# Sums of exponentials over agents: TensorE products with ones replaced by GpSimd reductions in pairs 6 to 25

## The chip, the cores and the metric

One Trainium2 chip, one of its cores. The metric is the device time of one execution in microseconds (us), measured from outside the program; three executions of the kernel before gave 986.49, 987.38 and 988.31 us. Times inside the kernel come from one profiled execution.

## The reference

Two batches of 12480 queries, keys and values with 128 channels, and 49 agents per batch, all float32. Then a feed-forward layer with 2048 hidden units and a leaky rectifier follows.

```
a2k     = softmax(agents @ k.T / sqrt(128))      # over the keys
agent_v = a2k @ v                                # 49 x 128
q2a     = softmax(q @ agents.T / sqrt(128))      # over the 49 agents
x       = q2a @ agent_v                          # 24960 x 128
h       = x @ w_in
out     = (max(h, 0) + alpha * min(h, 0)) @ w_out
```

## The kernel before, in words

The kernel never forms x. For each batch it folds agent_v into the first layer's weights, `sa` and `sb` (a value and what rounding left of it), so that h is the exponentials of the query scores times `sab`. The softmax of a query needs a division by the sum of its 49 exponentials; since the layer is positively homogeneous that division is done last, on the output rows.

The 24960 queries are cut in 52 groups of 480, and two groups make a **pair** k (0 to 25). A pair's tiles are 128 x 960: group 2k in the first 480 columns, group 2k+1 in the other 480. Partitions 0 to 63 hold the agents once and partitions 64 to 127 hold them again (49 are real, the others give exp = 0), so that two products with 64 rows each can go through the two halves of TensorE at the same time.

The main loop runs over 416 **steps** s, eight for each group, 16 for each pair; pair k begins at step s0 = 16 k. In step s the loop issues, in this order: what was put in `first` for the step (by `pre`), `g1(s + 2)`, what was put in `plan` for the step (by `at`), and `g2(s)`. Each engine works through its own instructions in that order, so the order of the text is the schedule.

- `g1` (lines 958 to 978): six products (64 rows, 480 columns each) into the two halves of a PSUM tile `h` (two such tiles), then ScalarE's `rh` = relu(h) (L974) and VectorE's `rl`, what rounding left of it (L975). L975 has one operand in PSUM and one in SBUF.
- `g2` (980 to 1008): twelve products of `rh` and `rl` into the group's accumulator (L990). In a group's last step three more products (L1001), ScalarE's copy (L1006) and VectorE's sum (L1007) close the group.
- The output of group g: `o_take` (a 32 x 32 block transpose on VectorE, L1012), `o_scale` (VectorE, times the reciprocal, L1017: two operands in SBUF) and `o_store` (four DMAs on SyncE's queue, L1035), at steps (g+1)*8 plus 4, 5 and 6, from `OUT`.
- The softmax of pair k, steps relative to s0 from `CHAIN`: `q_transpose` (VectorE, -18), `q_hi` (ScalarE) and `q_lo` (VectorE, two operands in SBUF, L845; both -16), `q_logits` (eight products, -14), `q_take` (ScalarE copy, -13), `q_swap` (two DMAs on SyncE's queue that swap the halves, L883, -13), `q_add` (VectorE, L890, -11), `q_max` (GpSimd's reduction over the partitions, L894, -10), `q_sub` (VectorE, L899, -7), `q_exp_hi` and `q_exp` (ScalarE, -6 and -5), `q_split` (VectorE, two operands in SBUF, L912, -5), `q_sum` (four products with a matrix of ones, L923, +4), `q_spread` (ScalarE copies the sums out of PSUM, L933, and a DMA on SyncE's queue puts them in the order of the output, L939; +5) and `q_rec` (three small instructions on VectorE, L946 to L951, +10).

Beside the pairs the keys of the second batch are worked on in steps 16 to 88 and its values in steps 96 to about 190 (`KEYS`, `VALUES`: `k_exp_a` L618, `v_split` L609 and `k_exp_c` L632 on VectorE, with two operands in SBUF each); steps 189 to 206 fold them into the second batch's weights. Pairs 1 to 5 lie mostly beside the keys, 6 to 12 beside the values, and 13 to 25 have the loop to themselves (called the late pairs below).

Of the kernel before, what the change touches and what calls it, by code (L numbers as in the profile page):

```python
# [9 lines left out]
F32 = mybir.dt.float32  # L10
F32R = mybir.dt.float32r
U32 = mybir.dt.uint32
AF = mybir.ActivationFunctionType
ALU = mybir.AluOpType
# [9 lines left out]
VALUES = ((((0, 3, 1, 1), (3, 1, 4, 4)), 6), (((3, 0, 7, 8), (2, 8, 5, 6)), 10))  # L24
FOLD = (189, 195, 198, 202, 205, 206)
CHAIN = (-18, -16, -16, -14, -13, -13, -11, -10, -7, -6, -5, -5, 4, 5, 10)
CHAIN_0 = (-19, -18, -18, -11, -9, -6, 1, 6, 10, 15, 17, 19)
CHAIN_1 = (-14, -13, -13, -11, -10, -10, -10, -10, -8, -7, -5, -5, 4, 5, 10)
EARLY = (1, 3, 6, 6)
OUT = (4, 5, 5)  # L30


LAGS = (7, 12, 17, 20, 21, 24)
# [22 lines left out]
def kernel(  # L56
# [11 lines left out]
    nc = tc.nc  # L68
# [4 lines left out]
    P = 128  # L73
    HALF = 64
    NF = DFF // P
    GT = 480
    TB = GT // 32
# [13 lines left out]
    SCALE = 1.0 / math.sqrt(C)  # L91
# [5 lines left out]
    p1 = ctx.enter_context(tc.tile_pool(name="p1", bufs=1))  # L97
    p2 = ctx.enter_context(tc.tile_pool(name="p2", bufs=2))
# [11 lines left out]
    def pair_tile(name, i=None):  # L110

        i = (step[0] // NM + 1) % 2 if i is None else i
        return late[i].tile([P, 2, 512], F32, tag="x", name=name)
# [21 lines left out]
    padb = const.tile([P, 1], F32, name="padb")  # L135
# [654 lines left out]
    NGT = B * NG  # L790
    gq = {}
# [20 lines left out]
    def flat(t):  # L812
        return t.rearrange("p h n -> p (h n)")
# [90 lines left out]
        gq["mh", k] = m  # L904

    def q_exp(k):
        e = gq["e", k] = gq.pop(("s", k))
        nc.scalar.activation(out=e, in_=e, func=AF.Exp, bias=padb, scale=SCALE)

    def q_split(k):  # L910
        m = p2.tile([P, 2, GT], F32R, tag="qml", name=f"qml{k}")
        nc.vector.tensor_tensor(out=m, in0=gq["e", k], in1=gq["mh", k], op=ALU.subtract)  # L912
        mh = gq.pop(("mh", k))
        gq.pop(("e", k))
        gq["mhl", k] = (m, mh)
        for i in range(2):
            gq["M", 2 * k + i] = (mh[:, i, :], m[:, i, :])

    def q_sum(k):
        t = gq["sum_ps", k] = pair_tile(f"qsum{k}")  # L920
        for n, x in enumerate(gq.pop(("mhl", k))):
            for i, (r0, r1) in enumerate(TILES):
                nc.tensor.matmul(  # L923
                    t[:, i, 0:GT], lhsT=ones[r0:r1, :], rhs=x[r0:r1, i, :],
                    start=n == 0, stop=n == 1,
                )

    def q_spread(k):
        if "sums" not in gq:
            t = gq["sums"] = p1m.tile([P, 1024], F32, tag="qsum", name="qsum")  # L930
            nc.gpsimd.memset(t[:, 2 * GT :], 1.0)
        t = gq["sums"]
        nc.scalar.copy(  # L933
            out=t[:, 0 : 2 * GT].rearrange("p (h n) -> p h n", h=2),
            in_=gq.pop(("sum_ps", k))[:, :, 0:GT],
        )

        x = p1m.tile([P, 32], F32, tag="qx", name=f"qx{k}")
        nc.sync.dma_start(  # L939
            out=x, in_=t.rearrange("(c o) (i j) -> c o i j", c=4, j=32)[:, 0, :, :]  # L940
        )
        gq["sum", k] = x

    def q_rec(k):
        t = p1m.tile([P, 32], F32, tag="qst", name=f"qst{k}")
        nc.vector.transpose(out=t, in_=gq.pop(("sum", k)))  # L946
        r = p2.tile([P, 2, TB, 1], F32, tag="qr", name=f"qr{k}")
        nc.vector.tensor_scalar(
            out=r.rearrange("p h t o -> p (h t o)"), in0=t[:, 0 : 2 * TB], scalar1=1e-9, scalar2=None, op0=ALU.add
        )  # L950
        nc.vector.reciprocal(out=r, in_=r)  # L951
        for i in range(2):
            gq["r", 2 * k + i] = r[:, i]
# [68 lines left out]
    def o_store(g):  # L1022
# [14 lines left out]
    q_chain = [  # L1037
        q_transpose, q_hi, q_lo, q_logits, q_take, q_swap, q_add, q_max,
        q_sub, q_exp_hi, q_exp, q_split, q_sum, q_spread, q_rec,
    ]  # L1040

# [5 lines left out]
    with tc.manual_schedule():  # L1047
# [10 lines left out]
        def at(s, f, *a):  # L1058
            plan.setdefault(s, []).append((f, a))
# [27 lines left out]
        at(q0 + PREPS[1], prep_queries, 1)  # L1087
        for j, f in zip(CHAIN_0, q_chain[:12]):
            at(q0 + j, f, 0)
# [4 lines left out]
        for n in range(7):  # L1094
            load, ops = (load_win, narrow_win) if n < 4 else (load_wo, narrow_wo)
            s = SLABS[n]
# [11 lines left out]
        def more():  # L1108
            f = next(loads, None)
            if f is not None:  # L1110
                f[1](*f[2:])
            return f

        while n_in < N_IN:
            f = more()
            n_in += f[1] not in (q_load_rows, load_alpha, load_late)
        for s in range(max(plan) + 1):
            for f, a in plan.pop(s, ()):
                f(*a)
                if f.__name__ == "total" or f in (k_turn, k_mix):  # L1120
                    while True:
                        f = more()
# [5 lines left out]
        p1m = ctx.enter_context(tc.tile_pool(name="p1m", bufs=1))  # L1128
# [19 lines left out]
        def pre(s, f, *a):  # L1148
            first.setdefault(s, []).append((f, a))

        for i2 in range(NGT // 2):
            s0 = 2 * NM * i2
            if i2 == 0:
                at(10, q_sum, 0)
                pre(11, q_spread, 0)
                at(13, q_rec, 0)
                continue
            steps = CHAIN if i2 > 1 else CHAIN_1
            if i2 > 1:
                at(max(0, s0 - LEADS[2]), q_load, i2)  # L1160
            for f, i in zip(q_chain, steps):
                (pre if f in (q_take, q_swap, q_spread) else at)(s0 + i, f, i2)
        for g in range(NGT):
            s0 = g * NM
            at((g + 1) * NM + OUT[0], o_take, g)
            d = OUT[1 if g % 2 == 0 or g == NGT - 1 else 2]
            at((g + 1) * NM + d, o_scale, g)
            at((g + 1) * NM + d + 1, o_store, g)

# [25 lines left out]
        for c, (lo, hi) in enumerate(parts):  # L1195
            s0 = VALUES_FROM + c // len(VALUES) * 16
            steps, av = VALUES[c % len(VALUES)]
# [58 lines left out]
```

## Time and profile before

| what | value |
|---|---|
| executions, median (lowest to highest) | 987.38 us (986.49 to 988.31) |
| the profiled execution, first to last instruction (its span) | 985.9 us; no other time of it is listed |
| TensorE (PE) busy | 971.7 us, 99% |
| VectorE (DVE) busy | 837.7 us, 85% |
| ScalarE (ACT) busy | 626.4 us, 64% |
| GpSimd (POOL) busy | 89.8 us, 9% |

The profile page has the busy time of each engine, the chain of work that ended last, and the costliest groups of instructions by line. The trace behind it answers for one line, one tile, one stretch of time. A timeline's columns are start, duration, engine, line, operation, output<-inputs, shape, count, and in brackets how long the engine stood idle before and for whom it waited. "x2" is two instructions merged in one row.

### The profile page before, as it was taken

What the parts mean: (1) busy time and instruction counts of PE and PEld (TensorE: products, weight loads), DVE (VectorE), ACT (ScalarE), POOL (GpSimd) and SP (SyncE); (2) the same over time, 40 slices, a digit from 0 to 9 for tenths busy, and PEclk for the clock granted to TensorE, in tenths of its full rate; (3) what the DMA queues carried; (4) which work ended last, traced back from release to release, by engine and by line L of the source; (5) the groups of instructions that cost most, each with busy time, mean ns of one, the idle gap of its engine ahead of it and who ended that gap; (6) DMA issues with size and microseconds to landing.
All of it is one profiled execution on the core that took longest, in us unless ns stands there. A gap on an engine that the chain in (4) does not pass through costs nothing.

```text
span 985.9 us, 21716 instructions
## 1 busy us (share of the span) xinstructions
PE 971.7 (99%) x9046; PEld 927.0 (94%) x9046; DVE 837.7 (85%) x1054; ACT 626.4 (64%) x779; POOL 89.8 (9%) x67
## 2 busy tenths in 40 slices
PE   8989999999999999999999999999999999999997
PEld 5658999999989999999987999999999999999997
DVE  7887988998899999999987788788878887888775
ACT  5765655655667767777765666666666666666563
POOL 0011011011011011001101101100110111011100
PEclk9999999999999999999999999999999999999999
DMA  9933354444234234234312222212221223121201
GB/s 342 361 51 63 65 84 87 81 70 88 42 75 80 62 73 95 45 70 95 65 31 44 42 51 41 53 37 46 52 53 31 42 55 56 35 41 33 42 11 31
DMA packets 281027, 69.51 MB, mean 71 GB/s; under 512 B 259119, under 2 KB 273953, under 8 KB 280929
## 3 DMA queue, kind: packets, MB, share of 16 engines
q1 hardware_dynamic: 279937, 68.00, 33.0%
q8 instruction: 71, 1.16, 0.5%
q10 hardware_dynamic: 992, 0.12, 0.1%
q14 instruction: 27, 0.22, 0.1%
HBM read 42.59 MB, written 12.78 MB: 56 GB/s over the span
## 4 chain that ended last, share of the span: by engine, by line
PE 94%; DVE 2%; DMA 2%; ACT 1%; issue 0%; SPq 0%; ACTq 0%
PE acc L990 55%; PE h L968 27%; PE lg L864 2%; PE kl L552 2%; PE acc L1001 2%; PE av L650 1%; PE qsum L923 1%; DMA kw<-in_k_dram 1%; DMA win<-in_moe_w_in_dram 1%; PE a_ps L726 0%; DVE red L414 0%; PE avw L471 0%; PE ktp L388 0%; PE lin_ps L784 0%; PE etp L451 0%
## 5 line engine op out<-in xcount | busy, mean ns | idle before, releaser
L975 DVE SCALAR_TENSOR_TENSOR rl<-h,rh 128x960 fp32r<-128x960 f32 x416 | 478.2, 1150 | 123.1 <-ACT rh L974 120.8
L974 ACT ACTIVATE rh<-h 128x960 fp32r<-128x960 f32 x416 | 404.3, 972 | 270.1 <-PE h L968 262.1
L968 PE MATMUL h<-qmh,sab 64*128 64x480 f32 x1664 | 401.3, 378 | 0.7 <-DVE rl L975 0.5
L990 PE MATMUL acc<-rh,wl 64*128 64x480 f32 x1664 | 400.3, 378 | 0.0
L990 PE MATMUL acc<-rh,wh 64*128 64x480 f32 x1664 | 398.0, 375 | 0.0
L990 PE MATMUL acc<-rl,wh 64*128 64x480 f32 x1664 | 313.2, 377 | 0.0
L968 PEld LDWEIGHTS h<-qmh,sab 64*128 64x128 f32 x1664 | 247.2, 185 | 7.5 <-DVE rl L975 2.5
L990 PEld LDWEIGHTS acc<-rh,wl 64*128 64x128 f32 x1664 | 246.9, 184 | 5.9 <-issue 2.3
L990 PEld LDWEIGHTS acc<-rh,wh 64*128 64x128 f32 x1664 | 247.6, 184 | 2.9
L990 PEld LDWEIGHTS acc<-rl,wh 64*128 64x128 f32 x1664 | 223.6, 184 | 3.2
L968 PE MATMUL h<-qml,sab 64*128 64x480 f32 x832 | 222.7, 377 | 0.0
L894 POOL PARTITION_ALL_REDUCE qm<-qs x26 | 85.6, 3293 | 768.0 <-DVE qs L890 731.3
L968 PEld LDWEIGHTS h<-qml,sab 64*128 64x128 f32 x832 | 128.0, 185 | 1.7 <-DVE qml L912 0.2
L1006 ACT COPY os<-acc 128x480 f32<-128x480 f32 x52 | 29.2, 561 | 33.8 <-PE acc L1001 33.6
L1007 DVE TENSOR_TENSOR os<-acc,os 128x480 f32<-128x480 f32 x52 | 33.9, 651 | 2.7 <-ACT os L1006 2.4
L1012 DVE STREAM_TRANSPOSE ot<-os 128x480 f32<-128x480 f32 x52 | 34.7, 668 | 0.0
L903 ACT ACTIVATE qmh<-qs,padb 128x960 fp32r<-128x960 f32 x26 | 28.5, 1097 | 9.2 <-DVE qs L899 9.2
L1017 DVE TENSOR_TENSOR ot<-ot,qr 128x480 f32<-128x480 f32 x52 | 33.6, 645 | 0.1
L899 DVE TENSOR_TENSOR qs<-qs,qm 128x960 f32<-128x960 f32 x26 | 29.8, 1148 | 0.5 <-POOL qm L894 0.5
L890 DVE TENSOR_TENSOR qs<-qs,qw 128x960 f32<-128x960 f32 x25 | 28.7, 1148 | 1.7 <-DMA qw<-qs 1.7
L912 DVE TENSOR_TENSOR qml<-qs,qmh 128x960 fp32r<-128x960 f32 x26 | 29.8, 1148 | 0.0
L827 DVE STREAM_TRANSPOSE qt<-qin 128x960 f32<-128x960 f32 x25 | 29.2, 1167 | 0.0
(172 smaller groups left out, 802.8 us busy)
## 6 DMA issues: line engine op xcount, KB each, us to landing
out_dram<-ot SPq DMA_DIRECT2D x206, 60.0 KB
qin<-in_q_dram SPq DMA_DIRECT2D x200, 60.0 KB
qw<-qs SPq DMA_DIRECT2D x50, 240.0 KB
kw<-in_k_dram SPq DMA_DIRECT2D x12, 512.0 KB
vw<-in_v_dram SPq DMA_DIRECT2D x12, 512.0 KB
kb<-in_k_dram SPq DMA_DIRECT2D x96, 64.0 KB
v<-in_v_dram SPq DMA_DIRECT2D x24, 256.0 KB
win<-in_moe_w_in_dram SPq DMA_DIRECT2D x4, 512.0 KB
```

What stands on the lines that cost most here:

```text
L827: nc.vector.transpose(out=flat(t), in_=gq.pop(("in", k)).rearrange("p h t i -> p (h t i)"))
L894: nc.gpsimd.partition_all_reduce(flat(t), flat(gq["s", k]), P, ReduceOp.max)
L899: nc.vector.tensor_tensor(out=t, in0=t, in1=gq.pop(("m", k)), op=ALU.subtract)
L912: nc.vector.tensor_tensor(out=m, in0=gq["e", k], in1=gq["mh", k], op=ALU.subtract)
L968: nc.tensor.matmul(h[:, u, 0:GT], lhsT=w[a][r0:r1, f0 : f0 + P], rhs=x[r0:r1, :], start=n == 0, stop=n == 2,)
L974: nc.scalar.activation(out=rh, in_=h[:, :, 0:GT], func=AF.Relu)
L975: nc.vector.scalar_tensor_tensor(out=rl, in0=h[:, :, 0:GT], scalar=0.0, in1=rh, op0=ALU.max, op1=ALU.subtract)
L990: nc.tensor.matmul(acc[:, i, 0:GT], lhsT=a[r0:r1, 2 * m + u, :], rhs=x[r0:r1, u, :], start=m == 0 and n == 0, stop=False,)
L1006: nc.scalar.copy(out=t, in_=acc[:, 0, 0:GT])
L1007: nc.vector.tensor_tensor(out=t, in0=acc[:, 1, 0:GT], in1=t, op=ALU.add)
L1012: nc.vector.transpose(out=t.rearrange("p t i -> p (t i)"), in_=oo.pop(g))
L1017: nc.vector.tensor_tensor(out=t, in0=t, in1=gq.pop(("r", g)).to_broadcast([P, TB, 32]), op=ALU.mult)
```

## The change

For pairs 6 to 25 (`POOL_FROM = 6`) the sum over the agents is no longer four products with ones on TensorE, copied out of PSUM by ScalarE. `q_exp` writes its exponentials to the buffer "qm" instead of over the scores, and `q_sum` lets GpSimd add them over all 128 partitions into the same SBUF tile `qsum` that ScalarE's copy filled. As the agents stand there twice, `q_rec` multiplies by 0.5. In front of the reduction GpSimd copies one column of `q_split`'s output (the gate), so that the reduction starts only when `q_split` is done. `q_sum` moves from s0 + 4 to s0 - 5 and `q_spread` from s0 + 5 to s0 + 1. The output scaling and stores of the even groups 10 to 48 move four steps later, from (g+1)*8 + 5 and 6 to + 9 and 10, which is steps 1 and 2 of the next pair. No tile moves to another address.

```diff
+CHAIN_P = (-18, -16, -16, -14, -13, -13, -11, -10, -7, -6, -5, -5, -5, 1, 10)
+POOL_FROM = 6
-OUT = (4, 5, 5)
+OUT = (4, 5, 9)
...
     def q_exp(k):
-        e = gq["e", k] = gq.pop(("s", k))
-        nc.scalar.activation(out=e, in_=e, func=AF.Exp, bias=padb, scale=SCALE)
+        s = e = gq.pop(("s", k))
+        if k >= POOL_FROM:
+            e = p1.tile([P, 2, GT], F32, tag="qm", name=f"qe{k}")
+        gq["e", k] = e
+        nc.scalar.activation(out=e, in_=s, func=AF.Exp, bias=padb, scale=SCALE)
...
+    def sums():
+        if "sums" not in gq:
+            t = gq["sums"] = p1m.tile([P, 1024], F32, tag="qsum", name="qsum")
+            nc.gpsimd.memset(t[:, 2 * GT :], 1.0)
+        return gq["sums"]
+
     def q_sum(k):
+        e = gq.pop(("e", k))
+        if k >= POOL_FROM:
+            m, _ = gq.pop(("mhl", k))
+            gate = p2.tile([P, 1], F32, tag="none", name=f"gate{k}")
+            nc.gpsimd.tensor_copy(gate, m[:, 1, GT - 1 : GT])
+            nc.gpsimd.partition_all_reduce(sums()[:, 0 : 2 * GT], flat(e), P, ReduceOp.add)
+            return
...
     def q_spread(k):
+        t = sums()
+        if k < POOL_FROM:
+            nc.scalar.copy(
+                out=t[:, 0 : 2 * GT].rearrange("p (h n) -> p h n", h=2),
+                in_=gq.pop(("sum_ps", k))[:, :, 0:GT],
+            )
...
-            out=r.rearrange("p h t o -> p (h t o)"), in0=t[:, 0 : 2 * TB], scalar1=1e-9, scalar2=None, op0=ALU.add
+            out=r.rearrange("p h t o -> p (h t o)"), in0=t[:, 0 : 2 * TB], scalar1=0.5 if k >= POOL_FROM else 1.0, scalar2=1e-9,
+            op0=ALU.mult, op1=ALU.add,
...
-            steps = CHAIN if i2 > 1 else CHAIN_1
+            steps = CHAIN_P if i2 >= POOL_FROM else CHAIN if i2 > 1 else CHAIN_1
...
-            d = OUT[1 if g % 2 == 0 or g == NGT - 1 else 2]
+            late_scale = g % 2 == 0 and 2 * POOL_FROM - 2 <= g < NGT - 2
+            d = OUT[2 if late_scale else 1]
```

## Rows read from the trace of the kernel before

**Rows 1.** The page: busy time of the engines, and the chain that ended last.
```profile
PE 971.7 (99%) x9046; PEld 927.0 (94%) x9046; DVE 837.7 (85%) x1054; ACT 626.4 (64%) x779; POOL 89.8 (9%) x67
...
PE 94%; DVE 2%; DMA 2%; ACT 1%; issue 0%; SPq 0%; ACTq 0%
```

**Rows 2.** The cores: span and mean granted TensorE clock as a share of 2.4 GHz.
```profile
core 0: 985.9 us, clock 0.998
```

**Rows 3.** Groups by line, PE, 285 to 960 us (busy, mean ns | idle before).
```profile
L968 PE MATMUL h<-qmh,sab 64*128 64x480 f32 x1262 | 310.9, 377 | 0.0
```

**Rows 4.** Instructions on tile qsum, 285 to 960 us (ns: min/median/max).
```profile
L923 PE MATMUL qsum<-qml,ones x40: 372/378/380, 305.1 to 956.3; 64*128 64x480 f32 x40
...
L933 ACT COPY qsum<-qsum x20: 942/954/957, 307.3 to 957.4; 128x960 f32<-128x960 f32 x20
```

**Rows 5.** Timeline of PE around one pair's products with ones.
```profile
445.38 0.43 PE L968 MATMUL h<-qmh,sab 64*128 64x480 f32 x2
...
446.04 0.43 PE L923 MATMUL qsum<-qml,ones 64*128 64x480 f32 x2
446.26 0.42 PE L923 MATMUL qsum<-qmh,ones 64*128 64x480 f32 x2
446.48 0.42 PE L990 MATMUL acc<-rh,wl 64*128 64x480 f32 x2
```

**Rows 6.** Timeline of POOL, 750 to 800 us.
```profile
763.27 3.31 POOL L894 PARTITION_ALL_REDUCE qm<-qs  x1 [30.00 <-DVE qs L890]
796.58 3.32 POOL L894 PARTITION_ALL_REDUCE qm<-qs  x1 [30.00 <-DVE qs L890]
```

**Rows 7.** Timeline of SP, DVE and POOL, 85 to 95 us.
```profile
85.49 1.19 SPq L883 DMA_DIRECT2D qw<-qs  x2
...
90.00 1.16 DVE L890 TENSOR_TENSOR qs<-qs,qw 128x960 f32<-128x960 f32 x1 [1.18 <-DMA qw<-qs]
...
91.32 3.04 POOL L894 PARTITION_ALL_REDUCE qm<-qs  x1 [36.56 <-DMA qin<-in_q_dram]
...
94.40 1.16 DVE L899 TENSOR_TENSOR qs<-qs,qm 128x960 f32<-128x960 f32 x1 [0.54 <-POOL qm L894]
```

**Rows 8.** Timeline of POOL and DVE beside the values, 417 to 423 us.
```profile
417.14 3.31 POOL L894 PARTITION_ALL_REDUCE qm<-qs  x1 [27.15 <-DVE qs L890]
...
417.47 1.15 DVE L975 SCALAR_TENSOR_TENSOR rl<-h,rh 128x960 fp32r<-128x960 f32 x1
418.53 0.87 DVE L632 TENSOR_TENSOR e<-s,e 128x196 fp32r<-128x196 f32 x1
...
422.76 0.35 DVE L632 TENSOR_TENSOR e<-s,e 128x196 fp32r<-128x196 f32 x1
```

**Rows 9.** Timeline of DVE, SP in one late pair, 753 to 785 us.
```profile
753.70 1.16 DVE L975 SCALAR_TENSOR_TENSOR rl<-h,rh 128x960 fp32r<-128x960 f32 x1 [0.64 <-ACT rh L974]
...
754.58 1.12 SPq L883 DMA_DIRECT2D qw<-qs  x2
...
761.96 1.15 DVE L890 TENSOR_TENSOR qs<-qs,qw 128x960 f32<-128x960 f32 x1
...
763.71 1.94 SPq L1035 DMA_DIRECT2D out_dram<-ot  x4
...
774.27 1.15 DVE L912 TENSOR_TENSOR qml<-qs,qmh 128x960 fp32r<-128x960 f32 x1
...
778.04 0.64 DVE L1017 TENSOR_TENSOR ot<-ot,qr 128x480 f32<-128x480 f32 x1
...
784.16 1.15 DVE L845 TENSOR_TENSOR ql<-qt,qh 128x960 fp32r<-128x960 f32 x1
```

**Rows 10.** Timeline of DVE beside the values, steps 2 and 3 of one pair.
```profile
443.58 1.15 DVE L975 SCALAR_TENSOR_TENSOR rl<-h,rh 128x960 fp32r<-128x960 f32 x1
...
445.35 1.16 DVE L975 SCALAR_TENSOR_TENSOR rl<-h,rh 128x960 fp32r<-128x960 f32 x1 [0.35 <-ACT rh L974]
```

**Rows 11.** Waits, 255 to 300 us (us in total, times, longest).
```profile
PEld h L968 <- DVE rl L975: 0.8, 3, 0.3
```

More of the change, by code (lines that the diff above doesn't have):

```diff
@@ L913, in q_split @@
         mh = gq.pop(("mh", k))
-        gq.pop(("e", k))
         gq["mhl", k] = (m, mh)
@@ L928, in q_spread @@
     def q_spread(k):
[L929 to L936, printed above, removed]
+        t = sums()
[4 more added lines that the diff above has]
+            )
         x = p1m.tile([P, 32], F32, tag="qx", name=f"qx{k}")
```

## The prediction

> **What bounds the kernel now.** First the page: PE is busy 971.7 of 985.9 us and holds 94% of the chain that ended last; VectorE is busy 85%, ScalarE 64%, GpSimd 9% [rows 1]. A busy PE need not be a paced PE, so I asked three more views. The mean granted clock is 0.998 of 2.4 GHz, the upper of its two levels, so there is no clock to win or, with PE as busy as now, to lose [rows 2]. In the stretch where the changed pairs lie, PE's first products of a step stood idle 0.0 us over 1262 instructions, although they need VectorE's `rl` of two steps before [rows 3]. And the pace agrees with a count. A late pair lasts 796.58 - 763.27 = 33.31 us from one reduction to the next [rows 6]. By the code it has 16 x 18 products in `g1` and `g2`, 8 for the logits, 4 with ones and 6 that close two groups: 306. Two run side by side, which makes 153 slots, and 33.31 / 153 = 0.218 us a slot. The same slot stands in the timeline: 446.04, 446.26, 446.48 [rows 5]. So PE streams without holes, and a late pair is exactly as long as its slots. What takes slots out of PE takes time out of the kernel, as long as VectorE, ScalarE and the DMAs keep up with a pair that is shorter by that much.
>
> **What is removed.** The products with ones are two slots: from 446.04 to 446.48, 0.44 us; by the count 2 x 0.2177 = 0.435 us [rows 5, 6]. The row of the tile has 40 products with `qml` in 20 pairs, and as many with `qmh` [rows 4]. 20 x 0.435 = **8.7 us** off PE. With them go 20 copies of 0.954 us on ScalarE, 19 us [rows 4]; I cost them at nothing: ScalarE is busy 64% [rows 1], and nothing is late when it is less.
>
> **What is added on GpSimd.** 20 reductions of 128 x 960. The trace has only the max of that shape, 3.31 us; the add does not occur in it. Here the end of the span can be trusted: in pair 1 the reduction ends at 91.32 + 3.04 = 94.36 and `q_sub`, which waited for it, starts at 94.40 [rows 7]. The Trainium skill (Perfetto Trace Analysis, GPSIMD Engine Instruction) says the opposite, that a GpSimd span in a profile is unreliable and spacing should be used; the trace disagrees with it by no more than 0.04 us, and by that rule the true add could be longer than any row shows, which is the third rival. Nearest row 3.31 us; I take that. GpSimd stands idle 30.00 us ahead of each of its max reductions [rows 6], so one more of 3.3 us costs nothing by itself. The gate is a copy of one column, some 0.2 us on the same idle engine: nothing. What is queued behind it on GpSimd is the reduction and then memsets and the max of the next pair, five steps and more later.
>
> What could be hurt is VectorE. The rows show the collision: beside a max, L632, with two operands in SBUF, takes 0.87 us where it takes 0.35 alone, while L975, with one operand in PSUM, takes 1.15 either way [rows 8, 10]. So I looked for VectorE's instructions with two SBUF operands behind `q_split`. The split starts at 774.27 and ends at 775.42; then come `rl`, a transpose, `rl`, the output scaling of the even group at 778.04, `rl`, and the next with two SBUF operands is `q_lo` at 784.16 [rows 9]. The change takes just that scaling away from there. The reduction would run from about 775.6 to 778.9, which leaves 5.2 us to `q_lo`. Cost: nothing up to a length of 784.16 - 775.6 = 8.6 us, which is 2.6 times the max. Bounds for the reductions' cost: no gain, and the third rival above.
>
> **What is moved.** `o_scale` of 20 even groups goes to step 1 of the next pair. In a late pair VectorE idles 0.64 us ahead of the `rl` at 753.70, and the scaling is 0.64 us [rows 9]: it fits, nothing. Beside the values it is tighter. There the `rl` at 443.58 follows without an idle, ends at 444.73, and PE starts the products that need its PSUM tile at 445.38 [rows 5, 10]: 0.65 us of slack against 0.64 us of scaling. The next `rl` had waited 0.35 us, which swallows half of the delay [rows 10]. This holds for pairs 6 to 11; bounds 0 and 6 x 0.64 = 3.8 us; the slack covers it almost, so I take a loss of 0.4 us.
>
> In exchange, the stretch ahead of pair 6's products loses a scaling in its crowded place: the last keys there make PE wait 0.8 us for `rl` in three places [rows 11]. Bounds 0 and 0.8 us; I take a gain of 0.4 us, half. The two cancel.
>
> SyncE's queue: the four stores of the even group now stand just ahead of `q_swap`'s two DMAs. Stores issue in 1.94 us; with the scaling done at about 753.6 they end at 755.6, and the swap, issued at 754.58 before, is 1.0 us later [rows 9]. `q_add` uses it 7.4 us after issue [rows 9], and where VectorE did wait for it the whole way took 4.5 us [rows 7]. With q_add 0.4 us sooner, 1.5 us are left: nothing, and if that cover were gone VectorE would stand still at `q_add` with every `rl` behind it. `q_spread`'s DMA, now at step 1, waits for a reduction that ended 6 us before, so it holds nothing up; the stores behind it wait for the scaling as they did. `q_rec` keeps its count of instructions. Exponentials in "qm" are read by 779, and the next writer is the swap nine us later: nothing.
>
> **Sum.** -8.7 + 0.4 - 0.4 = -8.7 us. The profiled span of 985.9 becomes 977.2. No time of that execution beside its span is listed; the median of the runs, 987.38, is 1.5 us above the span, and I keep that difference: **978.7 us**, 0.9% faster.
>
> **Rivals.**
> First, VectorE pays for the moved scaling beside the values: all of 0.64 us in six pairs falls on PE, and the gain ahead of pair 6 does not come. 987.4 - 8.7 + 3.8 = 982.5 us. For it: an `rl` with no idle ahead [rows 10]. Against: 0.65 us of slack. 0.08.
>
> Second, nothing comes of it: PE's slots go, but VectorE then paces the pair (85% busy [rows 1]), and each 0.435 us comes back as a wait of `h` for `rl`: 987.4 us. For it: late pairs have places in which VectorE runs without a pause. Against: the products with ones stand where it idles, and the zero idle of [rows 3]. A change that does not do what it says, such as a reduction that waits until PE is through, would end here too. 0.07.
>
> Third, **slower**: the add takes over 8.6 us and so holds `q_lo` at 784.16. The logits follow `q_lo` on PE, so its delay goes straight to PE. By L632's ratio 0.87 / 0.35, `q_lo` would grow from 1.15 to 2.86 us, by 1.7, in 19 pairs (none follows the last): 32.5 - 8.7 = 23.8 us, 1011 us. It decides from about 8.6 us of reduction; below it costs nothing. For it: the add's length is in no row. Against: a max of that shape is 3.0 to 3.3 us in all rows [rows 6, 7, 8]. The Trainium skill (GPSIMD Engine Reference, Key points) has the rule: GpSimd shares its SBUF interfaces with VectorE and contends with instructions of two SBUF inputs; L632's row agrees. 0.05.
>
> **How the numbers follow.** The forecast has 0.80. Its own range is 977 (the whole 0.8 us ahead of pair 6 gained, nothing lost, and the 0.9 us by which the runs scatter) to 981 (a third of the exposed scaling and the scatter). To hold 8 in 10 with the doubts on my unseen terms, the range also takes in the first rival: 976.8 to 982.8. A measurement of this kernel can tell about 0.2%, 2 us, from no change. Faster by more: forecast and first rival, 0.88. Within: the second, 0.07. Slower: the third, 0.05.
>
> **What would show it.** Right: a late pair of 32.87 us from max to max, products with ones in 6 pairs only, 46 reductions of which 20 are adds near 3.3 us that start behind `q_split`, `q_lo` at 1.15 us, and PE's `h` still at no idle. Wrong: adds over 8.6 us or `q_lo` over 1.2 us; VectorE idle ahead of `q_add` for a DMA; or waits of `h` for `rl` that grow beside the values (first rival) or in late pairs (second).

## The result, and the profile after

The changed kernel takes 979.41 us (median of 4 runs, 979.03 to 979.79) against 987.74 us (4 runs, 986.49 to 988.31): ratio 0.9913, interval 0.9901 to 0.9925. The forecast was 978.7 us in a range of 976.8 to 982.8. The span of the profiled execution went from 985.9 to 978.0 us.

First the page of the changed kernel, the lines that answer to [rows 1, 3], with the two new groups of GpSimd:

```profile
PE 965.4 (99%) x8966; PEld 905.0 (93%) x8966; DVE 838.0 (86%) x1054; ACT 610.1 (62%) x759; POOL 207.9 (21%) x107
...
PE 94%; DVE 4%; ACT 1%; issue 1%; ACTq 0%
...
L984 PE MATMUL h<-qmh,sab 64*128 64x480 f32 x1664 | 398.7, 378 | 0.7 <-DVE rl L991 0.6
...
L935 POOL PARTITION_ALL_REDUCE qsum<-qe x20 | 114.9, 5747 | 0.0
...
L934 POOL COPY gate<-qml 128x1 f32<-128x1 f32 x20 | 3.8, 190 | 189.5 <-DVE qml L917 189.5
```

PE has 80 instructions fewer and holds the same 94% of the chain. ScalarE has 20 copies less. GpSimd is busy 118 us more, and none of it is on the chain. But one number is not what the forecast took: the addition lasts 5.75 us, not the 3.31 us of the maximum. (In the rows, `qml`, `h` and `qsum` are the tiles written or read, and `x20` counts instructions.)

Where the time went is read best from GpSimd's maximum, one for each pair. Here it is before pair 6, pair 14 and pair 25, in the timeline of the kernel before:

```profile
277.07 3.31 POOL L894 PARTITION_ALL_REDUCE qm<-qs  x1 [34.73 <-DVE qs L890]
...
563.36 3.31 POOL L894 PARTITION_ALL_REDUCE qm<-qs  x1 [35.02 <-DVE qs L890]
...
929.83 3.31 POOL L894 PARTITION_ALL_REDUCE qm<-qs  x1 [30.00 <-DVE qs L890]
```

and in that of the changed kernel, with one addition and its gate:

```profile
277.51 3.32 POOL L896 PARTITION_ALL_REDUCE qm<-qs  x1 [34.76 <-DVE qs L892]
...
560.76 3.31 POOL L896 PARTITION_ALL_REDUCE qm<-qs  x1 [15.58 <-DVE qs L892]
...
770.25 0.18 POOL L934 COPY gate<-qml 128x1 f32<-128x1 f32 x1 [8.91 <-DVE qml L917]
770.40 5.75 POOL L935 PARTITION_ALL_REDUCE qsum<-qe  x1
...
922.40 3.31 POOL L896 PARTITION_ALL_REDUCE qm<-qs  x1 [14.76 <-DVE qs L892]
```

Between the maxima of pairs 14 and 25 lie eleven late pairs with their products with ones: 366.47 us before, 361.64 after, 0.439 us less a pair. That is two slots (0.435 us by the count). Between those of pairs 6 and 14 lie eight pairs: 286.29 before, 283.25 after, 3.04 us less where two slots each would give 3.50; some 0.46 us were lost there, beside the values. Up to pair 6 the changed kernel is 0.44 us later, in a part that the change does not touch; over the traces that share this part, the maximum of pair 6 stands anywhere from 275.70 to 277.62 us. From it to the end of the span the kernel before takes 708.8 us and the changed one 700.5, 8.3 us less.

The timeline of VectorE and SyncE in a late pair answers to [rows 9]:

```profile
769.04 1.15 DVE L917 TENSOR_TENSOR qml<-qe,qmh 128x960 fp32r<-128x960 f32 x1
...
773.47 1.16 DVE L991 SCALAR_TENSOR_TENSOR rl<-h,rh 128x960 fp32r<-128x960 f32 x1 [0.59 <-ACT rh L990]
...
776.18 0.58 SPq L954 DMA_DIRECT2D qx<-qsum  x1
...
778.93 1.15 DVE L847 TENSOR_TENSOR ql<-qt,qh 128x960 fp32r<-128x960 f32 x1
...
781.06 0.65 DVE L1033 TENSOR_TENSOR ot<-ot,qr 128x480 f32<-128x480 f32 x1
...
781.74 2.31 SPq L1051 DMA_DIRECT2D out_dram<-ot  x4
784.14 1.12 SPq L885 DMA_DIRECT2D qw<-qs  x2
...
789.60 1.15 DVE L892 TENSOR_TENSOR qs<-qs,qw 128x960 f32<-128x960 f32 x1
```

The addition ends at 776.15, and 0.03 us later the DMA that needs it is issued. `q_lo` at 778.93 keeps its 1.15 us, with 2.8 us to spare. The stores hold the issue of the swap's DMAs up to 784.14; `q_add` at 789.60 finds the swapped halves there and does not wait. From the issue to `q_add` are 5.46 us left, where it was 7.38 before [rows 9].

### The profile page after: what moved, and what is told of

It reads as the page before. It is cut to its first block, busy times and chain, and to the rows that moved or that the text cites. A ratio compares the mean times of both kernels' runs of the same rounds, so it can differ in the third digit from the quotient of the medians.

```text
span 978.0 us, 21579 instructions
## 1 busy us (share of the span) xinstructions
PE 965.4 (99%) x8966; PEld 905.0 (93%) x8966; DVE 838.0 (86%) x1054; ACT 610.1 (62%) x759; POOL 207.9 (21%) x107
## 3 DMA queue, kind: packets, MB, share of 16 engines
q8 instruction: 70, 1.15, 0.5%
## 4 chain that ended last, share of the span: by engine, by line
PE 94%; DVE 4%; ACT 1%; issue 1%; ACTq 0%
PE acc L1006 56%; PE h L984 28%; PE lg L866 2%; PE kl L554 2%; PE acc L1017 2%; PE av L652 1%; DVE red L416 1%; PE a_ps L728 0%; PE ktp L390 0%; PE warm L205 0%; PE lin_ps L786 0%; DVE win L318 0%; PE qsum L940 0%; ACT ktw L393 0%; PE avw L473 0%
## 5 line engine op out<-in xcount | busy, mean ns | idle before, releaser
L984 PEld LDWEIGHTS h<-qmh,sab 64*128 64x128 f32 x1664 | 243.5, 185 | 11.5 <-DVE rl L991 3.1
L1006 PEld LDWEIGHTS acc<-rh,wl 64*128 64x128 f32 x1664 | 243.1, 184 | 8.9 <-issue 2.5
L1006 PEld LDWEIGHTS acc<-rh,wh 64*128 64x128 f32 x1664 | 244.1, 184 | 5.8
L1006 PEld LDWEIGHTS acc<-rl,wh 64*128 64x128 f32 x1664 | 219.9, 184 | 6.1
L984 PEld LDWEIGHTS h<-qml,sab 64*128 64x128 f32 x832 | 126.0, 185 | 3.3 <-DVE qml L917 0.2
L935 POOL PARTITION_ALL_REDUCE qsum<-qe x20 | 114.9, 5747 | 0.0
L934 POOL COPY gate<-qml 128x1 f32<-128x1 f32 x20 | 3.8, 190 | 189.5 <-DVE qml L917 189.5
```

What stands on the lines that cost most here:

```text
L935: nc.gpsimd.partition_all_reduce(sums()[:, 0 : 2 * GT], flat(e), P, ReduceOp.add)
L984: nc.tensor.matmul(h[:, u, 0:GT], lhsT=w[a][r0:r1, f0 : f0 + P], rhs=x[r0:r1, :], start=n == 0, stop=n == 2,)
L1006: nc.tensor.matmul(acc[:, i, 0:GT], lhsT=a[r0:r1, 2 * m + u, :], rhs=x[r0:r1, u, :], start=m == 0 and n == 0, stop=False,)
```

## The experiments

Each ratio is to executions of the kernel before made beside the experiment, with medians of 988.15, 988.04 and 987.81 us for the three groups of runs, so it is not the time divided by the 987.74 us above.

**The products with ones put back.** The products return at s0 + 4, into a tile that nobody reads; GpSimd still makes the sums and ScalarE's copies stay away.

```diff
...
+    def q_ones(k):
+        t = pair_tile(f"ones{k}")
+        for n, x in enumerate(gq.pop(("mhl", k))):
+            for i, (r0, r1) in enumerate(TILES):
+                nc.tensor.matmul(
+                    t[:, i, 0:GT], lhsT=ones[r0:r1, :], rhs=x[r0:r1, i, :],
+                    start=n == 0, stop=n == 1,
+                )
...
+            if i2 >= POOL_FROM:
+                at(s0 + 4, q_ones, i2)
```

> The changed kernel with the four products with ones put back at step s0 + 4 of pairs 6 to 25, into a PSUM tile that nobody reads; GpSimd still makes the sums, ScalarE's copy stays away. If the gain is TensorE's two slots a pair: the late pair goes from 32.86 back to 33.3 us and the time to 987.3 to 988.5 us. Rival, the gain came from ScalarE's 20 copies of 0.954 us or from the PSUM tile that came free sooner: the time stays under 984 us.

Measured: 988.39 us, ratio to the kernel before 1.0001 (0.9992 to 1.0011). The maxima of pairs 14 and 25:

```profile
562.85 3.32 POOL L896 PARTITION_ALL_REDUCE qm<-qs  x1 [16.01 <-DVE qs L892]
...
929.32 3.31 POOL L896 PARTITION_ALL_REDUCE qm<-qs  x1 [15.20 <-DVE qs L892]
```

366.47 us for eleven pairs, the kernel before to the hundredth. All else of the change is in this kernel, and the gain is gone: it is PE's slots and not ScalarE's copies. The products take a PSUM tile again, so the run by itself does not tell a wait for that tile from the slots; but in this stretch the view of the waits lists none of PE's, neither for the kernel before nor for this one.

**The maximum for the addition.** The result of the reduction is then the largest exponential and not their sum.

```diff
-            nc.gpsimd.partition_all_reduce(sums()[:, 0 : 2 * GT], flat(e), P, ReduceOp.add)
+            nc.gpsimd.partition_all_reduce(sums()[:, 0 : 2 * GT], flat(e), P, ReduceOp.max)
```

> The changed kernel with the maximum in place of the sum in the new reduction, so the division uses the largest exponential and not the sum. If the length of 5.75 us belongs to the addition: the 20 new reductions take 3.3 us. If the length is hidden: late pair 32.86 us and 978.5 to 980.3 us, as with the sum. Rival, the longer addition costs on the path: at least 0.1 us a pair less, 977 us or under. Rival on the length, it comes from what runs beside it at that place: the maximum takes 5 us or more there too.

Measured: 978.78 us, ratio 0.9905 (0.989 to 0.992); the new reductions take 3.03 to 3.04 us, and eleven late pairs 361.63 us (560.30 to 921.93), as with the addition. So 5.75 us belongs to the operation, not to its place, and 2.7 us more of GpSimd cost nothing where it stands. The row of one:

```profile
769.93 3.04 POOL L935 PARTITION_ALL_REDUCE qsum<-qe  x1
```

**The scaling left where it was.** The new reduction as in the change, the scaling and stores of the even groups at their old steps.

```diff
-OUT = (4, 5, 9)
+OUT = (4, 5, 5)
```

> The changed kernel with the output scaling and stores of the even groups left at their old steps, so that the scaling (two operands in SBUF) falls about 2.4 us after the start of the new reduction. If the shared access decides: the scaling grows from 0.65 to 1.5 to 3 us, PE waits for rl behind it (0.2 to 0.6 us of slack), 0.3 to 2 us a pair, 985 to 1015 us. Rival, a scaling with a broadcast operand is not held up: 0.65 us, and 978.6 to 979.4 us, since the small loss beside the values goes too.

Measured: 993.08 us, ratio 1.0055 (1.0038 to 1.0071): slower than before. In the timeline, the addition, the scaling, and PE's next `h`:

```profile
778.45 5.75 POOL L935 PARTITION_ALL_REDUCE qsum<-qe  x1
...
780.85 2.35 DVE L1033 TENSOR_TENSOR ot<-ot,qr 128x480 f32<-128x480 f32 x1
...
783.13 1.14 DVE L991 SCALAR_TENSOR_TENSOR rl<-h,rh 128x960 fp32r<-128x960 f32 x1
...
784.33 0.48 PE L984 MATMUL h<-qmh,sab 64*128 64x480 f32 x2 [0.31 <-DVE rl L991]
```

The scaling takes 2.35 us in place of 0.65, `rl` behind it is late, and PE waits for it. Eleven late pairs take 370.74 us (563.68 to 934.42), 0.83 us a pair more than the changed kernel. Without the moved scaling the change loses.

**The moved scaling alone**, in the kernel before, with its products.

```diff
-OUT = (4, 5, 5)
+OUT = (4, 5, 9)
...
-            d = OUT[1 if g % 2 == 0 or g == NGT - 1 else 2]
+            d = OUT[2 if g % 2 == 0 and 10 <= g < NGT - 2 else 1]
```

> The kernel before with the output scaling and stores of even groups 10 to 48 moved four steps later and nothing else. If the moved scaling costs what the prediction took: pairs 6 to 11 get 0.05 to 0.15 us longer each (before: 35.18 to 35.29), late pairs stay at 33.3 us, and the span grows by 0.4 us or less. First rival: 0.64 us in each of the six pairs, 3.8 us in all.

Measured: a single execution, 987.66 us, span 985.9; its time says nothing this fine, its stretches do. The maxima of pairs 6 and 14:

```profile
276.59 3.31 POOL L894 PARTITION_ALL_REDUCE qm<-qs  x1 [34.67 <-DVE qs L890]
...
563.37 3.31 POOL L894 PARTITION_ALL_REDUCE qm<-qs  x1 [35.02 <-DVE qs L890]
```

286.78 us where the kernel before has 286.29: 0.49 us lost beside the values, with nothing but the scaling and its stores moved. The waits of PE's weight loads for `rl` in these eight pairs show it. They come to 0.8 us in three places in the kernel before and to 0.9 in three in the run further down with the scaling at its old place; with the scaling moved they are longer, here and in the changed kernel (total in us, times, longest):

```profile
PEld h L968 <- DVE rl L975: 1.2, 5, 0.3
...
PEld h L984 <- DVE rl L991: 1.5, 7, 0.3
```

From pair 14 to 25 it has 366.47 us (563.37 to 929.84): in late pairs the move is free, as the 0.64 us of idle in [rows 9] had said.

**Without the gate.** The new reduction starts when the exponentials are there.

```diff
-            m, _ = gq.pop(("mhl", k))
-            gate = p2.tile([P, 1], F32, tag="none", name=f"gate{k}")
-            nc.gpsimd.tensor_copy(gate, m[:, 1, GT - 1 : GT])
+            gq.pop(("mhl", k))
```

> The changed kernel without GpSimd's one-column copy ahead of the new reduction, which then starts as soon as the exponentials are there, beside the split. If the shared access decides: the split (1.15 us, two operands in SBUF) grows by 1 to 4 us, every rl behind it is late, and the time is 985 to 1040 us. Rival, the gate does nothing: split 1.15 us, 979 to 980 us.

Measured: 1090.6 us, ratio 1.1035 (1.1015 to 1.1055), far over what any theory expected. In the timeline the reduction starts 0.03 us before the split:

```profile
693.20 5.75 POOL L933 PARTITION_ALL_REDUCE qsum<-qe  x1 [7.68 <-ACT qe L913]
693.23 5.23 DVE L917 TENSOR_TENSOR qml<-qe,qmh 128x960 fp32r<-128x960 f32 x1
```

The split takes 5.23 us in place of 1.15. That is 4.1 us; the eleven late pairs are each 5.8 us longer (604.65 to 1030.32, 425.67 us, against 361.64). The stretches around it show part of the rest. The columns are the stretch, its length, the busy time of PE, PEld, DVE, ACT and POOL with counts, the granted clock and the DMA's share:

```profile
693.00:699.00 6.00, 2.96 (x28) 2.31 (x24) 6.00 (x3) 1.94 (x3) 5.75 (x1) 1.00 0.00 0
699.00:701.00 2.00, 1.42 (x10) 1.23 (x12) 2.00 (x3) 0.32 (x1) 0.00 (x0) 0.80 0.05 8
701.00:721.00 20.00, 20.00 (x176) 18.17 (x174) 15.01 (x17) 10.74 (x12) 0.51 (x1) 0.93 0.18 39
```

PE is busy 2.96 of 6 us while VectorE is held, and behind that gap the granted clock is 0.80 and then 0.93 of 2.4 GHz, a mean over each stretch between the two levels, 1.2 and 2.4 GHz; over the whole run it is 0.958. The same columns for all eleven late pairs, of this run and of the changed kernel, tell the waiting from the clock:

```profile
604.65:1030.32 425.67, 385.85 (x3326) 354.39 (x3324) 348.75 (x331) 223.18 (x242) 99.77 (x22) 0.94 0.21 39
...
560.76:922.40 361.64, 361.64 (x3326) 360.83 (x3324) 302.48 (x331) 223.17 (x242) 101.33 (x33) 1.00 0.25 45
```

PE stands idle 425.67 - 385.85 = 39.8 us, 3.6 us a pair, and the view of the waits puts 39.8 us of PE, eleven times, down to `h` waiting for `rl`. The same 3326 products are busy 385.85 us in place of 361.64, 2.2 us a pair more, at a granted clock of 0.94 in place of 1.00; 361.64 / 0.94 would be 384.7. So of the 5.8 us about 3.6 are waiting and about 2.2 the clock.

**The addition made twice**, 11.6 us, so that it is under way when `q_lo` is due.

```diff
-            nc.gpsimd.partition_all_reduce(sums()[:, 0 : 2 * GT], flat(e), P, ReduceOp.add)
+            for _ in range(2):
+                nc.gpsimd.partition_all_reduce(sums()[:, 0 : 2 * GT], flat(e), P, ReduceOp.add)
```

> The changed kernel with the new reduction made twice in a row, 11.5 us from step s0 - 5, so that it is still running when q_lo of the next pair is due 8.7 us after the split. By the prediction's third rival: q_lo grows from 1.15 to about 2.9 us, the logits on PE come that much later, 1.3 to 1.7 us a pair, 1003 to 1012 us. If only the first part of each reduction holds the access and the second one's first part ends before q_lo: q_lo 1.15 us and 979 to 980.5 us.

Measured: 1003.54 us, ratio 1.0157 (1.0141 to 1.0173); a late pair lasts 34.17 us (eleven: 570.36 to 946.19), 1.29 us more than the changed kernel's. In the timeline:

```profile
787.91 11.60 POOL L936 PARTITION_ALL_REDUCE qsum<-qe  x2
...
796.22 2.80 DVE L847 TENSOR_TENSOR ql<-qt,qh 128x960 fp32r<-128x960 f32 x1
...
799.07 0.49 PE L866 MATMUL lg<-ql,aq 64*128 64x480 f32 x2 [1.06 <-DVE ql L847]
```

`q_lo` takes 2.80 us, where the third rival had 2.86, and PE waits 1.06 us for it ahead of the logits.

**What a reduction holds, and until when.** Three instructions of different lengths (the scaling, the split, `q_lo`) have now met an addition, and a fourth case is in the timeline of the changed kernel itself, where a multiplication with two SBUF operands that belongs to the values (L690) meets one. The second block is the same instruction in the kernel before, with no reduction beside it:

```profile
500.93 5.74 POOL L935 PARTITION_ALL_REDUCE qsum<-qe  x1
...
503.91 1.54 DVE L690 TENSOR_TENSOR x<-x,rs 98x256 f32<-98x256 f32 x1
```

```profile
506.21 0.42 DVE L688 TENSOR_TENSOR x<-x,rs 98x256 f32<-98x256 f32 x1
```

Counted from the addition's start, the scaling ends at 4.75 us, the split at 5.26, this one at 4.52 (`q_lo` met the second of two additions that stand in one row, whose start the row does not give; if it starts 5.75 us before the row's end at 799.51, `q_lo` comes to 4.11 by the same reckoning, an estimate). Take off what each needs alone (0.65, 1.15, 0.42): 4.10, 4.11, 4.10. The three started 0.03, 2.40 and 2.98 us into the addition, so they are not slowed in proportion. They stand until 4.1 us of the addition's 5.75 and then run at full speed. In [rows 8] the same reckoning gives 1.9 us of 3.31 for the maximum. If that is so, a scaling that starts 2.4 us into a maximum is not held at all:

```diff
-OUT = (4, 5, 9)
+OUT = (4, 5, 5)
...
-            nc.gpsimd.partition_all_reduce(sums()[:, 0 : 2 * GT], flat(e), P, ReduceOp.add)
+            nc.gpsimd.partition_all_reduce(sums()[:, 0 : 2 * GT], flat(e), P, ReduceOp.max)
```

> The maximum in place of the sum in the new reduction, and the output scaling of the even groups at its old place, 2.4 us after the reduction's start. If a reduction holds instructions with two SBUF operands only up to a point before its end (4.1 us of 5.75 for the sum, 1.6 to 1.9 of 3.3 for the maximum) and lets them run at full speed after it: the scaling takes 0.65 us, late pairs last 32.87 us, 978 to 979.5 us. Rival, they are slowed for as long as the reduction lasts: the scaling takes 1.2 us or more (its last 0.7 us beside the maximum), late pairs 33 us or more, 981 us or more.

Measured: 979.09 us, ratio 0.991 (0.9893 to 0.9926). In the timeline:

```profile
769.98 3.04 POOL L935 PARTITION_ALL_REDUCE qsum<-qe  x1
...
772.39 0.64 DVE L1033 TENSOR_TENSOR ot<-ot,qr 128x480 f32<-128x480 f32 x1
```

0.64 us, beside the last 0.6 us of the reduction: the hold ends before its span does. The eight pairs from 6 to 14 take 282.75 us (277.59 to 560.34) here, 3.54 less than before, so with the scaling at its old place nothing is lost beside the values.

**From pair 2 on.** Four pairs more, beside the keys.

```diff
-POOL_FROM = 6
+POOL_FROM = 2
```

> The changed kernel with GpSimd's sums from pair 2 on, four pairs more, beside the keys. If every pair's gain is its two slots: 4 x 0.435 = 1.7 us less than the changed kernel, 977.7 us. If the moved scaling or the 5.75 us of the addition collide with the keys' work on VectorE (PE has 0.2 to 0.5 us of slack there): the pairs 2 to 5 get longer, up to 1 us each, 979 to 983 us.

Measured: 991.33 us, ratio 1.0032 (1.0019 to 1.0046). From the maximum of pair 2 to that of pair 6 it takes 165.61 us (123.19 to 288.80) where the kernel before takes 154.58 (122.49 to 277.07). The timeline names neither collision that I had expected:

```profile
153.61 1.95 SPq L1051 DMA_DIRECT2D out_dram<-ot  x4
155.60 4.24 SPq L530 DMA_DIRECT2D kb<-in_k_dram  x8
...
159.40 0.71 DVE L540 STREAM_TRANSPOSE kt<-kb 128x512 f32<-128x512 f32 x1 [3.09 <-DMA kb<-in_k_dram]
159.94 1.16 SPq L885 DMA_DIRECT2D qw<-qs  x2
...
164.32 1.16 DVE L892 TENSOR_TENSOR qs<-qs,qw 128x960 f32<-128x960 f32 x1 [1.54 <-DMA qw<-qs]
```

It is SyncE's queue. The stores wait for the moved scaling, the keys' loads and the swap are queued behind them (the same eight loads are issued from 151.30 us on in the kernel before), and VectorE stands 3.09 us for keys and 1.54 us for the swap. So I left the scaling and moved only the stores, behind the swap:

```diff
-POOL_FROM = 6
+POOL_FROM = 2
...
-            at((g + 1) * NM + d + 1, o_store, g)
+            at((g + 1) * NM + d + (5 if late_scale else 1), o_store, g)
```

> GpSimd's sums from pair 2 on, with the four stores of the even groups another four steps later (after q_swap and the keys' loads on SyncE's queue), the scaling as in the changed kernel. If the queue's order cost pairs 2 to 4 their 3.8 us each: they come down from 42.5 us to 38.65 - 0.43 + 0.1, and the time is 977.5 to 979 us, 1 to 1.7 us under the changed kernel. Rival, VectorE's collisions beside the keys cost it: 40 us or more a pair, 983 us or more.

 

> The changed kernel itself, for the comparison on this chip: 978.8 to 980 us, late pairs 32.86 us.

Measured: 978.25 us, ratio 0.9904 (0.989 to 0.9919), and the changed kernel on the same chip 978.94 us, ratio 0.9912 (0.9897 to 0.9926). The queue now:

```profile
152.01 4.13 SPq L530 DMA_DIRECT2D kb<-in_k_dram  x8
156.24 1.16 SPq L885 DMA_DIRECT2D qw<-qs  x2
157.44 6.83 SPq L1051 DMA_DIRECT2D out_dram<-ot  x8
```

From pair 2 to 6 it takes 153.45 us (123.20 to 276.65), 1.13 us less than before, of 1.74 that two slots a pair would give. The traces show that gain; the times of the two kernels overlap (977.72 to 978.86 and 978.56 to 979.47), so between them it is only the best median, not a measured difference.

## Why the prediction was right

**The removed slots**: forecast 0.435 us a pair, measured 0.439 us in late pairs; putting them back takes the whole gain. The count of slots, which says that a pair is as long as its products, carried the forecast, and so the mechanism was right.

**The additions at nothing**: right in the cost, wrong in the size. The nearest row, the maximum's 3.31 us, was taken for an addition that takes 5.75 us, so one of the prediction's own signs of being right, additions near 3.3 us, did not come. The cost stayed at nothing because the place left room to `q_lo`, as the stated margin of 8.6 us had provided for. The prediction says of the scaling only that the change takes it away from there. With 5.75 us the gain rests on that move (993.08 us without it); with 3.04 us it would not have been needed (979.09 us).

**The moved scaling**: 0.4 us lost beside the values was forecast; 0.46 and, alone, 0.49 us were measured. The 0.4 had been taken between bounds of 0 and 3.8 us, so that it came this close is in part luck. In late pairs nothing, as forecast.

**The gain of 0.4 us ahead of pair 6** is the term that failed. The wait there is unchanged; this is the row of the waits of the changed kernel that answers to [rows 11] (total in us, times, longest):

```profile
PEld h L984 <- DVE rl L991: 0.8, 3, 0.3
```

The scaling that left stood behind the crowded place, not in it. In the timeline of the kernel before, the last of the three waits ends at 291.55 us, and the scaling starts after it:

```profile
291.55 0.19 PEld L968 LDWEIGHTS h<-qmh,sab 64*128 64x128 f32 x2 [0.31 <-DVE rl L975]
...
293.05 0.64 DVE L1017 TENSOR_TENSOR ot<-ot,qr 128x480 f32<-128x480 f32 x1
```

Without it VectorE idles 0.40 us at that place in the changed kernel, and PE's waits stay as they were. With this term at nothing the sum is -8.7 + 0.4 = -8.3 us. From pair 6 to the end the traces give 8.3 us. The medians differ by 8.33, but with the interval of the ratio that is 7.4 to 9.8 us, so they alone could not tell 8.3 from 8.7. The rest of what the forecast missed by is the median of the kernel before, 987.38 us of three executions then and 987.74 of four.

**SyncE's queue**: the swap was issued later and nothing waited, as forecast. The cover was thinner than the 1.5 us of the forecast: 5.46 us less the 4.5 us of [rows 7] leave 1.0, as the four stores took 2.31 us and not 1.94. The stretch beside the keys shows what the same order costs where loads stand behind the stores.

**The rivals.** The first was right in its mechanism, as the longer waits of `h` for `rl` beside the values show, and had 0.46 of its 3.8 us. The second fell with the eleven late pairs. The third came near for `q_lo` (2.80 us for 2.86) by a wrong rule, which is luck, and a pair paid 1.29 us where it had 1.7. The ratio 0.87 / 0.35 is no property of the collision: it is a wait until a fixed point, 4.1 us in an addition, which ends before the addition does, and the length at which it decides is therefore not 8.6 us but more.

The Trainium skill (GPSIMD Engine Reference, Key points) says that VectorE's instructions with two SBUF inputs contend with GpSimd. The runs agree as to which instructions these are: the split was held (5.23 us for 1.15), and `rl`, with one operand in PSUM, was not (1.16 us at 773.47, where the addition had started at 770.40).

## What to carry to other kernels

Where one engine streams without holes, count its slots: what leaves them can be gained in full (here 0.439 us for two slots of 0.218), as long as the replacement finds a place in which nobody it can hold up is due. In this kernel a GpSimd reduction held VectorE's instructions with two SBUF operands for most of its length (4.1 of 5.75 us, 1.9 of 3.31), so its place is chosen by what stands in the next microseconds on VectorE, and one operation's duration is not another's. When stores are moved to make room, look at what is queued behind them on the same queue.

## What the runs showed of the hardware that was not expected

- A reduction over the partitions of 128 x 960 takes 5.75 us as an addition and 3.03 to 3.32 us as a maximum.
- A VectorE instruction with two SBUF operands that starts beside it stands until 4.1 us of the addition, and runs at full speed for the rest; `rl`, with one operand in PSUM, keeps its 1.15 us (1.11 to 1.16 over the profile of the changed kernel).
- Without the one-column copy of 0.18 us the split starts 0.03 us too late and takes 5.23 us; the kernel then loses 10%. Of the 5.8 us that a late pair loses, about 3.6 are PE's wait and about 2.2 the clock, which behind the gap of PE was granted at a mean of 0.80 and then 0.93 of 2.4 GHz.
